# First feed-forward layer of a fused attention and mixing kernel: two blocks of hidden rows together, their 64-row products on two halves of the array

## The chip, the cores and the metric

The kernel runs on one core of one Trainium2 chip. The metric is the device time of one execution in microseconds. The time given for a kernel is the median of its runs. One execution was also recorded by the hardware profiler; the rows below are from it.

## What is computed

Three layers follow each other on `x` of shape (4, 4224, 192): a causal convolution with 7 taps for each head, a layer that mixes tokens with two 4224 x 4224 matrices, and a layer of rank-32 token mixing with a feed-forward network. The change touches the last one:

```python
def _moe2_ref(x, U, V, w_ch1, w_ch2):
    xt = x.transpose(0, 2, 1)
    h = xt @ U @ V
    u = x + h.transpose(0, 2, 1)
    ch = np.maximum(u @ w_ch1, 0.0) @ w_ch2
    return (u + ch).astype(np.float32)
```

`w_ch1` is 192 x 768, `w_ch2` 768 x 192. `d_model` is 192 = 128 + 64, so each contraction over it leaves 64 rows beside a full 128.

## The kernel before

The data lie transposed, features on the partitions and tokens along the free dimension. The four batches stand in two pairs (`p`). Of each pair the first batch's 128 rows are slot 0, the second's slot 2, and the two leftover 64 rows share slot 1, the first batch's in the upper half of the partitions (0 to 63), the second's in the lower half (64 to 127).

Every matrix product runs in fp32r, with each operand split into a high and a low part. A product is high by high, high by low and low by high, summed in PSUM. For the 64-row leftover, `parts_hi` and `parts_lo` build a slot (4 + b for batch b of the pair) that has the high part in one half and the low part in the other: high on top for b = 0, low on top for b = 1. The leftover weights stand in both halves, so one matmul over 128 rows gives (high + low) of the input by a weight.

Most of the span is the token mixing (`mix`, `group`, line 553). The feed-forward stage is the last sixth. `seq` lists its steps: 22 blocks `n` (11 chunks of 384 tokens by two pairs of batches), in each two batches `b`, in each six pieces `m` of 128 hidden rows, 264 steps in all. The order is written out by hand:

- `up(n, b, m)` makes one piece of the hidden layer: five matmuls of 384 columns into one PSUM bank of the pool `acc` (four banks, also used by `lift`): lines 818 and 819 the high weights by high and low input, 820 the low weights by high input, 821 the high leftover weights by slot 4 + b, 822 the low leftover weights by the same slot. ScalarE then takes the ReLU (824), VectorE the low part of it (825). `hid` has four buffers.
- `down`, two steps behind (`LAG`), multiplies the piece with the second layer: 840 and 841 into `ob`, 842 to 844 into `oa`.
- `lift` adds the rank-32 term to the input of the next block (one matmul, line 798, and an add on VectorE, line 800) at the steps in `LIFTS`: (0, 4), (0, 5) and (1, 0). `lift_split` splits that input: at b = 1, m = 1 `parts_hi` on ScalarE (603 to 605), at b = 1, m = 2 `parts_lo`, the large part on GpSimd (608), two small ones on VectorE (611, 614).
- `load_v` fetches and unpacks the next chunk of V. `finish` copies and adds the result (858, 859, 864, 870) and sends it out.
- `tail` holds what is left of the stage before and runs beside the first two steps: `m1[3]` transposes (665) and splits (669, 670), `m1[4]` multiplies with U (675), and `stack` prepares the rank-32 factor.

Of the kernel before, what the change touches and what calls it, by code (L numbers as in the profile page):

```python
# [10 lines left out]
F32 = mybir.dt.float32  # L11
F32R = mybir.dt.float32r
I32 = mybir.dt.int32
U16 = mybir.dt.uint16
AF = mybir.ActivationFunctionType
ALU = mybir.AluOpType
PSUM = bass.MemoryType.PSUM

P = 128
# [9 lines left out]
NM = DFF // P  # L29
BLOCKS = [1] * NS  # L30

COLS = 384
# [60 lines left out]
LIFTS = [(0, 4), (0, 5), (1, 0)]  # L93
# [20 lines left out]
def mix_kernel(ctx, tc, xT, wcv, wth, wtok, wch, uu, vv, w1, w2, outT):  # L114
    nc = tc.nc
    mm = nc.tensor.matmul

    def pool(name, bufs=1, side=None, space=None, stack=None):
        kw = dict(name=name, bufs=bufs, reuse_waits="tile")
        if side:  # L120
            kw["side"] = side
        if space is not None:
            kw["space"] = space
        return (stack or ctx).enter_context(tc.tile_pool(**kw))

    def f(ap):
        return ap.bitcast(F32)
# [47 lines left out]
    zp = pool("zp", bufs=4, side="right", stack=right)  # L175
    pp = pool("prep", side="right", stack=prep_st)
    ps_mm = pool("ps_mm", bufs=4, space=PSUM)
# [3 lines left out]
    y = [yt[:, :, o : o + w] for o, w in LATE]  # L181

    with tc.manual_schedule():
# [39 lines left out]
        n_chunks = len(pieces) // 2  # L223
# [20 lines left out]
        for h in range(2):  # L244
# [10 lines left out]
            out=wex, in0=wc_raw, in1=wmx.unsqueeze(2).to_broadcast([P, 2, TAPS]), op=ALU.subtract  # L255
# [10 lines left out]
            out=tap, in0=wex, in1=wsm.unsqueeze(2).to_broadcast([P, 2, TAPS]), op=ALU.mult  # L266
# [152 lines left out]
        def weight_part(t, g, q):  # L419

            if g < n_chunks:
                kb, n, _ = pieces[2 * g]
                if g >= n_chunks - len(LATE):

                    t = t[:, 8 : 8 + 4 * LSTEP]
                return t.rearrange("p (q k n) -> p q k n", q=2, k=2)[:, q, :kb, :n]

            return t[:, 2 * WSTEP * q + 16 : 2 * WSTEP * q + 16 + 2 * COLS]
# [172 lines left out]
        def parts_hi(q, src, p):  # L601

            nc.scalar.copy(q[0:64, 4, :], src[0:64, 3 * p + 1, :])
            nc.scalar.copy(q[64:128, 5, :], src[64:128, 3 * p + 1, :])
            nc.scalar.copy(q[:, 0:2, :], src[:, 3 * p : 3 * p + 3 : 2, :])  # L605
# [137 lines left out]
        m0, m1 = mixed[nmix - 2 :]  # L743
# [17 lines left out]
        c1 = (wh[n_chunks], wl[n_chunks])  # L761
# [6 lines left out]
        fo = pool("fin", stack=fin)  # L768
# [4 lines left out]
        def load_v(c, part):  # L773

            if c >= len(LATE):
                return
            if part == 0:
                vw = vraw[c] = vw_two[:, c % 2, :COLS, :]
                nc.sync.dma_start(out=vw, in_=v_columns(c))
            elif part == 1:  # L780
                unpack_parts(vraw[c])
            elif part == 2:
                unpack_join(vraw[c])
            else:
                v = late_fo["pool"].tile([P, COLS], F32R, name="vs", tag="vs", bufs=2)
                t = late_fo["pool"].tile([P, COLS], F32R, name="vt", tag="vt")
                split_v(c, words(vraw.pop(c), 1, F32), v, t)

        vraw = {}
        uq = {}  # L790

        def lift(n, j):

            if n >= nmix:
                return
            c, p = divmod(n, 2)
            h = ps_mm.tile([P, COLS], F32, name="acc", tag="acc")
            mm(h, pst[:, p, j * P : (j + 1) * P], vst[c], start=True, stop=True)
            d = y[c][:, 3 * p + j, :]
            nc.vector.tensor_tensor(out=d, in0=h, in1=d, op=ALU.add)  # L800

        def lift_split(n, part, eng=nc.gpsimd):
            if n >= nmix:
                return
            c, p = divmod(n, 2)
            if part == 0:
                uq[n] = zp.tile([P, 6, COLS], F32R, name="fq", tag="z")
                parts_hi(uq[n], y[c], p)
            else:
                parts_lo(uq[n], y[c], p, eng)  # L810

        hid = {}

        def up(n, b, m):
            q = uq[n]
            ps = ps_mm.tile([P, COLS], F32, name="acc", tag="acc")
            w = [weight_part(c1[part], n_chunks, h)[:, m * P : (m + 1) * P] for h in range(2) for part in range(2)]
            mm(ps, w[0], q[:, b, :], start=True, stop=False)  # L818
            mm(ps, w[0], q[:, 2 + b, :], start=False, stop=False)  # L819
            mm(ps, w[1], q[:, b, :], start=False, stop=False)  # L820
            mm(ps, w[2], q[:, 4 + b, :], start=False, stop=False)  # L821
            mm(ps, w[3], q[:, 4 + b, :], start=False, stop=True)  # L822
            h = hid[n, b, m] = fo.tile([P, 2, COLS], F32R, name="hid", tag="hid", bufs=4)
            nc.scalar.activation(h[:, 0, :], ps, AF.Relu)  # L824
            nc.vector.scalar_tensor_tensor(  # L825
                out=h[:, 1, :], in0=ps, scalar=0.0, in1=f(h[:, 0, :]), op0=ALU.max, op1=ALU.subtract
            )

        acc = {}

        def down(n, b, m):
            if m == 0:
                acc[n, b] = (
                    ps_p.tile([P, COLS], F32, name="oa", tag=f"acc{b}"),
                    ps_t.tile([P, COLS], F32, name="ob", tag="tr"),
                )
            oa, ob = acc[n, b]
            h = hid.pop((n, b, m))
            first, last = m == 0, m == NM - 1
            mm(ob, c2[:, m, 2, :], h[:, 0, :], start=first, stop=False)  # L840
            mm(ob, c2[:, m, 2, :], h[:, 1, :], start=False, stop=last)  # L841
            mm(oa, c2[:, m, 0, :], h[:, 0, :], start=first, stop=False)  # L842
            mm(oa, c2[:, m, 0, :], h[:, 1, :], start=False, stop=False)  # L843
            mm(oa, c2[:, m, 1, :], h[:, 0, :], start=False, stop=last)  # L844
# [4 lines left out]
        def finish(n, b, part):  # L849
            c, p = divmod(n, 2)  # L850
            if b == 0 and part == 0:
                outs[n] = late_fo["pool"].tile([P, 3, COLS], F32, name="ot", tag="ot", bufs=2)
            o = outs[n]
            oa, ob = acc[n, b]
            a, z = (0, 64) if b == 0 else (64, 0)
            dst = out3[:, 3 * p : 3 * p + 3, c * COLS : (c + 1) * COLS]
            if part == 0:
                nc.scalar.copy(o[a : a + 64, 1, :], ob[z : z + 64, :])
                nc.vector.tensor_tensor(
                    out=o[a : a + 64, 1, :], in0=ob[a : a + 64, :], in1=o[a : a + 64, 1, :], op=ALU.add  # L860
                )
            elif part == 1:
                if b == 1:
                    nc.vector.tensor_tensor(
                        out=o[:, 1, :], in0=o[:, 1, :], in1=y[c][:, 3 * p + 1, :], op=ALU.add
                    )
                    if n == nmix - 1:
                        nc.sync.dma_start(out=dst[:, 0:2], in_=o[:, 0:2, :])
            else:
                nc.vector.tensor_tensor(  # L870
                    out=o[:, 2 * b, :], in0=oa, in1=y[c][:, 3 * p + 2 * b, :], op=ALU.add
                )
                if b == 1:
                    first = 2 if n == nmix - 1 else 0
                    nc.sync.dma_start(out=dst[:, first:], in_=outs.pop(n)[:, first:, :])
# [9 lines left out]
        seq = [(n, b, m) for n in range(nmix) for b in range(2) for m in range(NM)]  # L885
        LAG = 2

        def post_done():
# [3 lines left out]
        tail = {  # L892
            0: [lambda: m1[4](0), lambda: m1[3](2)],
            1: [lambda: m1[4](1), lambda: m1[4](2), lambda: stack(1), post_done],
        }
        for i in range(len(seq) + LAG + 2):
            if i < len(seq):
                n, b, m = seq[i]
                up(n, b, m)
                for fn in tail.pop(i, ()):  # L900
                    fn()
                if n % 2 == 0 and b == 1 and m >= 3:
                    load_v(n // 2 + 1, m - 2)
                if n % 2 == 1 and b == 0 and m == 0:
                    load_v(n // 2 + 2, 0)
                if (b, m) in LIFTS:
                    lift(n + 1, LIFTS.index((b, m)))
                if b == 1 and m in (1, 2):
                    lift_split(n + 1, m - 1)
            if LAG <= i < len(seq) + LAG:  # L910
                down(*seq[i - LAG])
            for part in range(3):
                if 0 <= i - LAG - part < len(seq) and seq[i - LAG - part][2] == NM - 1:
                    finish(*seq[i - LAG - part][:2], part)
        fin.close()
        right.close()
        left.close()
# [62 lines left out]
```

## Time and profile before

| | |
|---|---|
| median of 3 runs | 3009.88 us (3009.52 to 3011.36) |
| profiled execution | 3011.35 us, its span 3009.6 us |
| mean granted TensorE clock | 0.995 |
| TensorE matmul, busy | 2960.8 us, 98% of the span |
| weight loads, busy | 2691.3 us, 89% |
| VectorE, busy | 2523.7 us, 84% |
| ScalarE, busy | 1570.8 us, 52% |
| GpSimd, busy | 275.3 us, 9% |
| feed-forward stage | about 2528 us to the end |

The profile is one execution of the program on the chip, times in microseconds from the start of the span. PE is TensorE's matmuls, PEld its weight loads, which overlap them, DVE is VectorE, ACT ScalarE, POOL GpSimd, SP SyncE. L822 is line 822 of the kernel. Matmuls are pipelined, and the ends of their records are modelled, so the distance of two starts says more than a record's length. Shares over the span average stages with different limits.

### The profile page before, as it was taken

Reading aid. Unit: us, or ns where it says so; the run is one execution under the profiler, and the core shown is the slowest. Engines: PE = TensorE matmul, PEld = TensorE weight load, DVE = VectorE, ACT = ScalarE, POOL = GpSimd, SP = SyncE. Lnnn points to the kernel's source line nnn. Section 1 sums busy time; section 2 is a strip of 40 time slices with the busy share of each in tenths; the row PEclk is TensorE's granted clock in tenths of the full one; section 3 lists DMA queues with packets and bytes.
Section 4 is the critical chain, followed back from the end, with each engine's and each line's share of the span. In section 5 each row is a group of like instructions: output and inputs, shape, how many; then the busy total and the mean of one; then the engine's idle time right before and its main releaser. Section 6 shows DMA issues by size and latency. Waiting matters only on the chain.

```text
span 3009.6 us, 38806 instructions
## 1 busy us (share of the span) xinstructions
PE 2960.8 (98%) x14884; PEld 2691.3 (89%) x14884; DVE 2523.7 (84%) x4147; ACT 1570.8 (52%) x2268; POOL 275.3 (9%) x245
## 2 busy tenths in 40 slices
PE   6999999999999999999999999999999998999999
PEld 5888888888888888888888888888889998999999
DVE  8799989898888888888989898889888997565655
ACT  7755555554555555454545454545455565444443
POOL 3210101000000000000001010000010000000000
PEclk9999999999999999999999999999999999999999
DMA  3433434343434343434343344333333221101110
GB/s 109 133 124 121 134 124 134 120 135 120 135 120 135 123 133 123 135 120 132 124 130 125 126 130 129 130 127 128 125 119 103 65 64 43 43 30 43 35 38 32
DMA packets 119002, 323.50 MB, mean 107 GB/s; under 512 B 6688, under 2 KB 40480, under 8 KB 118688
## 3 DMA queue, kind: packets, MB, share of 16 engines
q1 hardware_dynamic: 118816, 321.01, 33.1%
q8 instruction: 117, 1.92, 0.3%
q14 instruction: 69, 0.57, 0.1%
HBM read 308.01 MB, written 12.98 MB: 107 GB/s over the span
## 4 chain that ended last, share of the span: by engine, by line
PE 93%; DVE 4%; ACT 2%; issue 1%; DMA 0%; POOL 0%; DVEq 0%; POOLq 0%; ACTq 0%
PE acc L553 71%; PE ob L841 2%; PE ob L840 2%; PE oa L844 2%; PE oa L842 2%; PE acc L822 2%; PE acc L818 2%; PE acc L819 2%; PE acc L820 2%; PE oa L843 2%; PE acc L821 1%; DVE wraw L147 1%; PE pacc L675 1%; DVE wraw L150 1%; PE tr L665 1%; PE th L356 1%
## 5 line engine op out<-in xcount | busy, mean ns | idle before, releaser
L553 PE MATMUL acc<-whi,z 128*128 128x464 f32 (+2 forms) x7224 | 2131.4, 373 | 8.9 <-ACT yt L557 4.9
L553 PEld LDWEIGHTS acc<-whi,z 128*128 128x128 f32 x7224 | 1358.2, 188 | 174.8 <-ACT yt L557 7.6
L553 PE MATMUL acc<-wlo,z 128*128 128x464 f32 (+2 forms) x3612 | 1347.2, 373 | 3.0 <-POOL wlo L450 3.0
L553 PEld LDWEIGHTS acc<-wlo,z 128*128 128x128 f32 x3612 | 680.0, 188 | 89.8 <-POOL wlo L450 4.3
L559 DVE TENSOR_TENSOR yt<-acc,yt 128x464 f32<-128x464 f32 (+2 forms) x876 | 550.8, 634 | 221.9 <-PE acc L553 219.3
L447 ACT CAST whi<-wraw 128x928 fp32r<-128x928 f32 (+3 forms) x304 | 315.4, 1038 | 659.2 <-DVE wraw L150 658.9
L147 DVE TENSOR_SCALAR wraw<-wraw 128x928 uint16<-128x928 uint16 (+3 forms) x307 | 372.0, 1212 | 10.2 <-ACT wraw L143 6.1
L450 DVE TENSOR_TENSOR wlo<-wraw,whi 128x928 fp32r<-128x928 f32 (+2 forms) x290 | 371.8, 1282 | 1.0 <-ACT whi L447 1.0
L142 ACT ACTIVATE wraw<-wraw,consts 128x928 int32<-128x928 uint16 (+3 forms) x307 | 351.2, 1144 | 14.9 <-DMA wraw<-in_wtok 11.6
L150 DVE SCALAR_TENSOR_TENSOR wraw<-wraw 128x928 int32<-128x928 int32 (+3 forms) x307 | 344.9, 1123 | 10.6
L143 ACT ACTIVATE wraw<-wraw 128x928 f32<-128x928 f32 (+3 forms) x307 | 321.0, 1046 | 0.0
L316 DVE SCALAR_TENSOR_TENSOR xa<-xr,tap,xa 128x256 f32<-128x256 f32 (+1 forms) x768 | 301.6, 434 | 0.0
L403 POOL TENSOR_TENSOR z<-tz,z 128x384 fp32r<-128x384 f32 x120 | 123.9, 1032 | 1712.7 <-ACT z L400 1712.7
L825 DVE SCALAR_TENSOR_TENSOR hid<-acc,hid 128x384 fp32r<-128x384 f32 x264 | 146.8, 556 | 151.0 <-ACT hid L824 149.9
L824 ACT ACTIVATE hid<-acc 128x384 fp32r<-128x384 f32 x264 | 129.6, 491 | 255.0 <-PE acc L822 253.0
L400 ACT CAST z<-tz 128x384 fp32r<-128x384 f32 x130 | 66.7, 513 | 294.9 <-DVE tz L389 294.9
L818 PE MATMUL acc<-fq,whi 128*128 128x384 f32 x264 | 89.9, 341 | 5.5 <-ACT fq L605 5.5
L409 POOL TENSOR_TENSOR yt<-yt,xa 128x384 f32<-128x384 f32 x64 | 69.6, 1088 | 229.4 <-DVE xa L316 193.7
L844 PE MATMUL oa<-hid,cl 128*128 128x384 f32 x264 | 90.0, 341 | 0.0
L842 PE MATMUL oa<-hid,cl 128*128 128x384 f32 x264 | 89.8, 340 | 0.0
L840 PE MATMUL ob<-hid,cl 128*128 128x384 f32 x264 | 89.7, 340 | 0.0
L841 PE MATMUL ob<-hid,cl 128*128 128x384 f32 x264 | 89.7, 340 | 0.0
(216 smaller groups left out, 2792.0 us busy)
## 6 DMA issues: line engine op xcount, KB each, us to landing
wraw<-in_wtok SPq DMA_DIRECT2D x186, 928.0 KB, 4.7
wraw<-in_wtok SPq DMA_DIRECT2D x92, 960.0 KB, 4.9
wraw<-in_wtok SPq DMA_DIRECT2D x22, 768.0 KB, 4.3
xr<-in_xT SPq DMA_DIRECT2D x65, 201.0 KB, 2.6
outT<-ot SPq DMA_DIRECT2D x21, 576.0 KB, 2.9
vw<-in_vv SPq DMA_DIRECT2D x10, 384.0 KB, 3.9
wraw<-in_w SPq DMA_DIRECT2D x3, 768.0 KB, 4.3
ur<-in_uu SPq DMA_DIRECT2D x1, 1056.0 KB, 6.9
```

What stands on the lines that cost most here:

```text
L142: nc.scalar.activation(words(raw, 0), words(raw, 1, U16), AF.Identity, scale=2.0**-13, bias=consts[:, 3:4])
L143: nc.scalar.activation(words(raw, 1, F32), words(raw, 1, F32), AF.Copy, scale=2.0**-112)
L147: nc.vector.tensor_scalar(out=words(raw, 1, U16), in0=words(raw, 3, U16), scalar1=0x8000, scalar2=None, op0=ALU.bitwise_and)
L150: nc.vector.scalar_tensor_tensor(out=words(raw, 1), in0=words(raw, 1), scalar=3, in1=words(raw, 0), op0=ALU.logical_shift_left, op1=ALU.bi ...
L316: nc.vector.scalar_tensor_tensor(out=xa, in0=src, scalar=w, in1=xa, op0=ALU.mult, op1=ALU.add)
L447: nc.scalar.copy(hi, src)
L450: eng.tensor_tensor(out=weight_part(wl[g], g, q), in0=src, in1=f(hi), op=ALU.subtract)
L553: mm(ps, a, b[:, i + r, :], start=n == 0, stop=n == last)
L559: nc.vector.tensor_tensor(out=dst, in0=ps, in1=dst, op=ALU.add)
L818: mm(ps, w[0], q[:, b, :], start=True, stop=False)
L842: mm(oa, c2[:, m, 0, :], h[:, 0, :], start=first, stop=False)
L844: mm(oa, c2[:, m, 1, :], h[:, 0, :], start=False, stop=last)
```

## The change

`up` now takes two steps, m0 and m0 + 1. For each it runs the first four matmuls as before, into two banks. The fifth of each is now one over 64 rows: only the high part of the input by the low leftover weights, the first on the upper half of the array (rows 0 to 63), the second on the lower half (rows 64 to 127). Both read 384 columns and write all 128 partitions of their bank. Slot 4 + b has the high part in one half only, so the tile of a block gets a seventh slot with the high parts in the other halves, which two more ScalarE copies of 64 x 384 in `lift_split` fill. ReLU and low part of both pieces come after all ten matmuls. The loop goes in steps of two: `up` for a pair, then what stood beside the first and the second (`beside`), then `down` and `finish` for the two steps of the pair before. The low by low product of the leftover rows, which before came along in L822, is no longer computed.

```diff
--- before.py
+++ after.py
@@ -804,27 +804,35 @@
                 return
             c, p = divmod(n, 2)
             if part == 0:
-                uq[n] = zp.tile([P, 6, COLS], F32R, name="fq", tag="z")
-                parts_hi(uq[n], y[c], p)
+                q = uq[n] = zp.tile([P, 7, COLS], F32R, name="fq", tag="z")
+                parts_hi(q, y[c], p)
+                nc.scalar.copy(q[64:128, 6, :], y[c][0:64, 3 * p + 1, :])
+                nc.scalar.copy(q[0:64, 6, :], y[c][64:128, 3 * p + 1, :])
             else:
                 parts_lo(uq[n], y[c], p, eng)
 
         hid = {}
 
-        def up(n, b, m):
+        def up(n, b, m0):
             q = uq[n]
-            ps = ps_mm.tile([P, COLS], F32, name="acc", tag="acc")
-            w = [weight_part(c1[part], n_chunks, h)[:, m * P : (m + 1) * P] for h in range(2) for part in range(2)]
-            mm(ps, w[0], q[:, b, :], start=True, stop=False)
-            mm(ps, w[0], q[:, 2 + b, :], start=False, stop=False)
-            mm(ps, w[1], q[:, b, :], start=False, stop=False)
-            mm(ps, w[2], q[:, 4 + b, :], start=False, stop=False)
-            mm(ps, w[3], q[:, 4 + b, :], start=False, stop=True)
-            h = hid[n, b, m] = fo.tile([P, 2, COLS], F32R, name="hid", tag="hid", bufs=4)
-            nc.scalar.activation(h[:, 0, :], ps, AF.Relu)
-            nc.vector.scalar_tensor_tensor(
-                out=h[:, 1, :], in0=ps, scalar=0.0, in1=f(h[:, 0, :]), op0=ALU.max, op1=ALU.subtract
-            )
+            sums = []
+            for m in (m0, m0 + 1):
+                ps = ps_mm.tile([P, COLS], F32, name="acc", tag="acc")
+                w = [weight_part(c1[part], n_chunks, h)[:, m * P : (m + 1) * P] for h in range(2) for part in range(2)]
+                mm(ps, w[0], q[:, b, :], start=True, stop=False)
+                mm(ps, w[0], q[:, 2 + b, :], start=False, stop=False)
+                mm(ps, w[1], q[:, b, :], start=False, stop=False)
+                mm(ps, w[2], q[:, 4 + b, :], start=False, stop=False)
+                sums.append((ps, w[3]))
+            for t, (ps, w) in enumerate(sums):
+                r = slice(64 * t, 64 * t + 64)
+                mm(ps, w[r], q[r, 4 + b if t == b else 6, :], start=False, stop=True)
+            for t, (ps, _) in enumerate(sums):
+                h = hid[n, b, m0 + t] = fo.tile([P, 2, COLS], F32R, name="hid", tag="hid", bufs=4)
+                nc.scalar.activation(h[:, 0, :], ps, AF.Relu)
+                nc.vector.scalar_tensor_tensor(
+                    out=h[:, 1, :], in0=ps, scalar=0.0, in1=f(h[:, 0, :]), op0=ALU.max, op1=ALU.subtract
+                )
 
         acc = {}
 
@@ -893,25 +901,30 @@
             0: [lambda: m1[4](0), lambda: m1[3](2)],
             1: [lambda: m1[4](1), lambda: m1[4](2), lambda: stack(1), post_done],
         }
-        for i in range(len(seq) + LAG + 2):
-            if i < len(seq):
-                n, b, m = seq[i]
-                up(n, b, m)
-                for fn in tail.pop(i, ()):
-                    fn()
-                if n % 2 == 0 and b == 1 and m >= 3:
-                    load_v(n // 2 + 1, m - 2)
-                if n % 2 == 1 and b == 0 and m == 0:
-                    load_v(n // 2 + 2, 0)
-                if (b, m) in LIFTS:
-                    lift(n + 1, LIFTS.index((b, m)))
-                if b == 1 and m in (1, 2):
-                    lift_split(n + 1, m - 1)
-            if LAG <= i < len(seq) + LAG:
-                down(*seq[i - LAG])
-            for part in range(3):
-                if 0 <= i - LAG - part < len(seq) and seq[i - LAG - part][2] == NM - 1:
-                    finish(*seq[i - LAG - part][:2], part)
+        def beside(i):
+            n, b, m = seq[i]
+            for fn in tail.pop(i, ()):
+                fn()
+            if n % 2 == 0 and b == 1 and m >= 3:
+                load_v(n // 2 + 1, m - 2)
+            if n % 2 == 1 and b == 0 and m == 0:
+                load_v(n // 2 + 2, 0)
+            if (b, m) in LIFTS:
+                lift(n + 1, LIFTS.index((b, m)))
+            if b == 1 and m in (1, 2):
+                lift_split(n + 1, m - 1)
+
+        for i0 in range(0, len(seq) + LAG + 2, 2):
+            if i0 < len(seq):
+                up(*seq[i0])
+                for i in (i0, i0 + 1):
+                    beside(i)
+            for i in (i0, i0 + 1):
+                if LAG <= i < len(seq) + LAG:
+                    down(*seq[i - LAG])
+                for part in range(3):
+                    if 0 <= i - LAG - part < len(seq) and seq[i - LAG - part][2] == NM - 1:
+                        finish(*seq[i - LAG - part][:2], part)
         fin.close()
         right.close()
         left.close()
```

## Rows read from the trace of the kernel before

**Rows 1.** The page: busy us (share of the span) and instructions of an engine.
```profile
PE 2960.8 (98%) x14884; PEld 2691.3 (89%) x14884; DVE 2523.7 (84%) x4147; ACT 1570.8 (52%) x2268; POOL 275.3 (9%) x245
```

**Rows 2.** Three stretches of the feed-forward stage: length, busy times (instructions), granted clock, DMA.
```profile
2600.00:2700.00 100.00, 100.00 (x575) 100.00 (x574) 58.19 (x109) 44.58 (x88) 9.26 (x5) 1.00 0.11 38
2700.00:2800.00 100.00, 100.00 (x574) 100.00 (x573) 58.20 (x110) 43.10 (x85) 7.42 (x4) 1.00 0.12 42
2800.00:2900.00 100.00, 100.00 (x575) 100.00 (x574) 59.22 (x111) 47.36 (x93) 9.27 (x5) 1.00 0.09 33
```

**Rows 3.** Who waited for whom, 2600 to 2900 us: us in total, times, longest.
```profile
POOL fq L608 <- ACT fq L605: 274.8, 14, 19.8
ACT hid L824 <- PE acc L822: 159.4, 140, 1.4
DVE hid L825 <- ACT hid L824: 92.8, 112, 1.2
```

**Rows 4.** Instructions in order of time, one step: start us, length us, engine, line.
```profile
2780.12 0.33 PE L821 MATMUL acc<-fq,whi 128*128 128x384 f32 x1
2780.29 0.34 PE L822 MATMUL acc<-fq,wlo 128*128 128x384 f32 x1
2780.29 0.19 PEld L840 LDWEIGHTS ob<-hid,cl 128*128 128x128 f32 x1
2780.46 0.34 PE L840 MATMUL ob<-hid,cl 128*128 128x384 f32 x1
...
2780.66 0.49 ACT L824 ACTIVATE hid<-acc 128x384 fp32r<-128x384 f32 x1 [1.42 <-PE acc L822]
```

**Rows 5.** Weight loads of two lines: ns min/median/max, first and last start us.
```profile
L822 PEld LDWEIGHTS acc<-fq,wlo x264: 187/188/330, 2530.0 to 3001.4; 128*128 128x128 f32 x132
...
L675 PEld LDWEIGHTS pacc<-u2s,cz x132: 133/137/223, 2299.4 to 2533.8; 128*64 128x64 f32 x132
```

**Rows 6.** In order of time: L675 (64 columns) between transposes; x3 merges three.
```profile
2303.67 0.49 PE L665 MATMUL tr<-ident,yt 128*128 128x128 f32 x3
2303.91 0.59 PE L675 MATMUL pacc<-u2s,cz 128*64 128x384 f32 x2
2304.34 0.49 PE L665 MATMUL tr<-ident,yt 128*128 128x128 f32 x3
2304.58 0.42 PE L553 MATMUL acc<-whi,z 128*128 128x384 f32 x1
2304.84 0.34 PE L553 MATMUL acc<-wlo,z 128*128 128x384 f32 x1
...
2303.67 0.25 PEld L665 LDWEIGHTS tr<-ident,yt 128*128 128x128 f32 x2
...
2304.16 0.34 PE L675 MATMUL pacc<-u2s,cz 128*64 128x384 f32 x1
```

**Rows 7.** The group of all L675: count, busy us, mean ns, idle before.
```profile
L675 PE MATMUL pacc<-u2s,cz 128*64 128x384 f32 x132 | 38.6, 370 | 3.1 <-DVE u2s L670 2.8 <-ACT u2s L669 0.3
```

**Rows 8.** What writes the split input fq: ns min/median/max, first and last start us.
```profile
L603 ACT CAST fq<-yt x22: 499/506/515, 2526.3 to 2974.4; 64x384 fp32r<-64x384 f32 x22
L604 ACT CAST fq<-yt x22: 507/511/511, 2526.8 to 2974.9; 64x384 fp32r<-64x384 f32 x22
L605 ACT CAST fq<-yt x22: 832/837/837, 2527.3 to 2975.4; 128x768 fp32r<-128x768 f32 x22
...
L608 POOL TENSOR_TENSOR fq<-yt,fq x21: 1836/1854/1857, 2546.7 to 2976.4; 128x768 fp32r<-128x768 f32 x21
```

**Rows 9.** Groups, 2600 to 2900 us: count, busy us, mean ns, idle before.
```profile
L825 DVE SCALAR_TENSOR_TENSOR hid<-acc,hid 128x384 fp32r<-128x384 f32 x168 | 93.5, 556 | 93.5 <-ACT hid L824 92.8
L824 ACT ACTIVATE hid<-acc 128x384 fp32r<-128x384 f32 x168 | 82.5, 491 | 160.8 <-PE acc L822 159.4
...
L800 DVE TENSOR_TENSOR yt<-acc,yt 128x384 f32<-128x384 f32 x42 | 23.0, 547 | 0.0
...
L858 ACT COPY ot<-ob 64x384 f32<-64x384 f32 x28 | 13.3, 474 | 0.7
```

**Rows 10.** In order of time, the start of the feed-forward stage, TensorE.
```profile
2528.21 0.69 PE L818 MATMUL acc<-fq,whi 128*128 128x384 f32 x1 [5.51 <-ACT fq L605]
...
2531.34 0.84 PE L665 MATMUL tr<-ident,yt 128*128 128x128 f32 x3
...
2533.42 0.85 PE L675 MATMUL pacc<-u2s,cz 128*64 128x384 f32 x4
```

## What the change is predicted to do, before it was run

> **What bounds the kernel now.** I read the share of each engine first, then stretches of the stage that the diff touches, then who waited for whom there, then single instructions. TensorE is busy for 98% of the span [rows 1], but that number alone says little, so the stage decides. The feed-forward stage runs from about 2528 us to the end. Three stretches of 100 us from its middle show TensorE with no gap, at a granted clock of 1.00 (2.4 GHz), VectorE at 58 to 59% and ScalarE at 43 to 47% [rows 2]. In the list of waits of the same 300 us TensorE doesn't appear as a waiter; ScalarE waits for its products, and GpSimd for ScalarE [rows 3]. So in this stage time is the number of matmul slots times the length of a slot. The rows with 575, 574 and 575 matmuls in 100 us each give 0.174 us a slot, and two neighbours start 2780.29 and 2780.46 [rows 2, 4]. A weight load starts together with the matmul before it (the load of L840 at 2780.29, with the matmul of L822) and is hidden in it [rows 4].
>
> **The part that is to gain.** A step (one of 12 pieces of 128 hidden rows for a pair of batches) is five slots in up and five in down. The fifth in up (L822) multiplies the low part of the leftover 64 weight rows with high and low parts of the input, though only the high part matters. The change makes it a product of 64 rows, and runs those of two neighbouring steps in the two halves of the array. There are 264 steps, so 132 pairs, and for each pair two slots of 0.174 us become one shared stretch. Were the two products exactly side by side, 132 x 0.174 = 22.9 us would go.
>
> The trace of before has no matmul on 64 rows, so what the shared stretch costs has to be bounded. Three things can spoil it: the second weight load, a changeover between the full and the halved array, and that the halves don't overlap at all.
>
> *The second load.* Loads of 128 columns last 188 ns and of 64 columns 137 ns [rows 5]; the difference, 51 ns for 64 columns, makes 102 ns for 128, the rest being a fixed delay. The three short transposes say the same from another side: their loads and matmuls follow each other every 0.11 us, although 128 columns at 2.4 GHz stream in 0.053 us [rows 6]. So a load holds its path for 0.102 us, and a matmul can follow its load by 0.11 us. Take T as the start of the last full product of the pair. If both loads go one after the other from T, the upper half's matmul starts at T+0.174 (when the full one is through), the lower half's at T+0.102+0.110 = T+0.212. It streams until T+0.386, and the load for L840, which needs both halves, starts at T+0.212 and is ready at T+0.322, in time. L840 starts at T+0.386 where it starts at T+0.522 today: 0.136 us saved a pair, 18.0 us in all. If the second load must wait until the first half's matmul has begun, as every load of before waits for the matmul ahead of it [rows 4], the lower half starts at T+0.174+0.110 = T+0.284 and L840 at T+0.458: 0.064 us saved, 8.4 us. I take the first: the load of the lower half touches no weights that the upper half's matmul needs, whereas in before every load writes where the next but one would.
>
> *The changeover.* The nearest rows are the products of L675, which fill only 64 columns and stand between transposes of the full array [rows 6]. From the third transpose (about 2303.89, as the rows put the three 0.11 apart) to the second L675 at 2304.16 is 0.27 us, and 0.11 + 0.174 = 0.28 is what two slots need without any changeover; from there to the next transpose is 0.18, an ordinary slot; and back at L553 the two starts 2304.84 minus about 2304.56 are 0.28 again. Over all 132 of them the records are 370 ns long against 340 ordinarily, 4 us in total, with 3.1 us of idle time [rows 7]. So changing the number of columns costs about nothing here. It is a change of columns and not of rows, so it isn't proof, and the other end of the bound is an empty array: a matmul record is 0.34 us from start to written result [rows 4], so a changeover that waits for the last result costs 0.34 - 0.174 = 0.166 us, twice a pair. I take zero, by L675, and keep the other end as a rival.
>
> Here two rules of the Trainium skill stand against each other. TensorEngine Tiling (Array Packing), section Tiling Modes, states that changing the tiling mode, as against only the tile, drains TensorE; by that rule the changeover would be paid twice a pair, and L675 shows nothing of the kind, though no run here has yet changed the number of rows. TensorE: Matmul & The Clock Gate, Part 3, has small tiles start about 4 ns apart; by that figure the estimate would be 132 x (0.174 - 0.004) = 22.4 us.
>
> **What it adds beside TensorE.** Two copies of 64x384 on ScalarE for each of 22 blocks, at 0.51 us as L603 and L604 [rows 8], 22.4 us in all, in an engine that is over half idle in this stage [rows 2]. I cost them at nothing, and follow them where the queue is fullest: the pair b=1, m=0 and 1. Count from its first matmul. Eight full slots end at 1.39, the ReLU starts 0.37 after its product's start (2780.29 to 2780.66 [rows 4]), so two ReLUs of 0.49 end at about 2.75; VectorE's two subtractions of 0.56 end at 3.4 and the add of the third lift at 3.95 [rows 9]. L605 waits for that add, since lift and copies now stand in one iteration, so ScalarE does L603 and L604 until 3.8, L605 (0.84) until 4.8, the new copies until 5.8 and L858 (0.47) until 6.3 [rows 8, 9]. The next pair's first ReLU was ready at 5.3: it is 1.0 late, and its hidden tile is complete at about 7.4. TensorE wants that tile after one more pair, at about 8.6. GpSimd's L608 (1.85) [rows 8] starts at 4.8 and ends at 6.7, and the next block's first product comes at about 10. So 1.2 us are left. Were that cover gone, up to 22 x 1.0 = 22 us would show.
>
> Taking two pieces together also makes PSUM tighter. Each iteration takes two of the four acc banks, and three lifts in six iterations take one each. The tightest spot is the pair after the first two lifts, which takes the banks of the pair before: their last reader ends at 3.4, TensorE comes back at 1.6 + 2 x 0.174 + 10 x 0.174 = 3.7. 0.3 us are left, and each 0.1 us missing would cost 2.2 us over 22 blocks. SyncE's transfers (load_v and the output) and GpSimd's queue keep their order; they move by one step at most, and none is waited for here [rows 3].
>
> At the start of the stage there is a small loss. Today five matmuls stand between the transposes of L665 and the four L675 that need their result (2531.34 and 2533.42 [rows 10]). With ten products ahead of both, only two L675 (0.35 to 0.65 us) stand between, while ReLU 0.49, ReLU 0.49, copy 0.48 and a subtraction of 0.56 come before the result is there. TensorE waits about 1 us once (0 to 2 us). The first L818 still waits only for L605, since the new copies stand behind it [rows 8, 10]. At the end nothing changes: the last pair's second hidden tile is ready about 2.0 us after its product begins and used after 2.8.
>
> **The sum.** -18.0 + 1.0 = -17.0 us. The profiled execution took 3011.35 us, 3009.6 of it span, which is 1.5 us over the median of three; so 2994.4 us against it, and 2993 us against the median of 3009.88.
>
> **Rivals.** All from the median. (a) The loads overlap entirely, or a little better than I have it: -22.9 + 1.0, 2988; I count it into the forecast, whose own range is 2986 to 2998. (b) The second load waits for the first half's matmul: -8.4 + 1.0, 3002.5. For it speaks that no load of before runs two ahead [rows 4]. (c) The halves don't overlap and the 64 rows cost a whole slot each: 3011, so the change wouldn't do what it says. Nothing in the trace speaks against it, as before has no such pair. (d) The slower side: each changeover waits until the array is empty. The halves then start at T+0.340 and L840 at T+0.680, 0.158 us later than today; 132 x 0.158 + 1.0 = 21.9 us, 3032. It decides from 0.087 us a changeover, at which the gain of 0.174 is eaten up. Against it speaks L675, for it that a whole product's result leaves the array 0.34 us after its start while the halves would already be taking over [rows 4, 6]. This is what the page on tiling named above would lead to. (e) The loads wait for the empty array too: T+0.340, both loads until T+0.55, empty again at T+0.89, a load, T+1.00: 0.48 us a pair, 3074.
>
> **How the numbers follow.** Chances: forecast with (a) 0.38, (b) 0.17, (c) 0.17, (d) 0.20, (e) 0.08. The slower cases hold 0.28, more than 2 in 10, so the range reaches to (d) and leaves out (e) alone: 2986 to 3034. It covers the unknown price of a changeover between zero and an emptied array. About 0.2%, 6 us, is what a measurement here can tell from no change. Faster takes the forecast and most of (b): 0.53. The same takes (c) and the rest of (b): 0.19. Slower is (d) and (e): 0.28.
>
> **What would show it.** In a profile after, the last product of a pair's first half and of the second should start about 0.04 us apart, and L840 0.17 after the second; 0.11 apart means (b), 0.17 apart (c). A gap of more than 0.2 us ahead of the first or behind the second means (d), and loads that begin only behind that gap (e). In the middle of the stage 300 us hold 168 steps today [rows 9], 3.571 us a pair; they should hold 175, 3.435 us a pair. Waits of TensorE for ScalarE or VectorE once a block would show that the copies or the banks were mis-costed, and a wait of about 1 us near 2533 us the loss at the start. The prediction fails first with the changeover, which no row of before can price.

## The result, and the profile after

The changed kernel takes 3037.93 us (median of 4, 3036.38 to 3039.07), the kernel before 3009.78 us: a ratio of 1.0091, with a 95% interval of 1.0078 to 1.0104. It is 28.2 us slower. The forecast was 2993 us, and the time lies above the range, between the rivals (d), 3032, and (e), 3074. The profiled execution took 3036.38 us, 3034.6 of it span.

The stretches of the feed-forward stage, with the columns of [rows 2], show fewer matmuls in the same time, at the same clock of 1.00, and weight loads busy for 88% where they were busy throughout:

```profile
2600.00:2700.00 100.00, 100.00 (x545) 88.77 (x544) 53.49 (x105) 43.05 (x90) 7.32 (x4) 1.00 0.11 38
2700.00:2800.00 100.00, 100.00 (x544) 88.33 (x543) 52.74 (x103) 46.05 (x95) 9.18 (x5) 1.00 0.09 32
2800.00:2900.00 100.00, 100.00 (x545) 88.77 (x544) 52.41 (x103) 43.37 (x91) 7.32 (x4) 1.00 0.09 32
```

TensorE's busy share is still 100%, so it hides the loss. The records of matmuls reach over it. The loss is in the share of the loads, and in the list of waits of 2600 to 2900 us (us in total, times, longest), where the weight loads now wait, for nothing that the profile names:

```profile
ACT hid L832 <- PE acc L829: 145.4, 60, 3.2
...
PEld acc L829 <- issue: 19.4, 79, 0.2
...
PEld ob L848 <- issue: 9.9, 53, 0.2
...
PEld acc L798 <- issue: 4.8, 26, 0.2
```

79 pairs lie in these 300 us. 79 times the loads of the 64-row products (L829) wait 0.25 us, and 79 times (53 + 26) the load behind them does, 0.19 us. TensorE itself waits for ScalarE or VectorE nowhere. One pair in order of time, matmuls first, then loads (start us, length us):

```profile
2783.41 0.33 PE L824 MATMUL acc<-fq,wlo 128*128 128x384 f32 x1
2783.58 0.34 PE L825 MATMUL acc<-fq,whi 128*128 128x384 f32 x1
2783.85 0.44 PE L829 MATMUL acc<-fq,wlo 64*128 64x384 f32 x2
2784.22 0.44 PE L848 MATMUL ob<-hid,cl 128*128 128x384 f32 x1
2784.50 0.34 PE L849 MATMUL ob<-hid,cl 128*128 128x384 f32 x1
...
2783.41 0.19 PEld L825 LDWEIGHTS acc<-fq,whi 128*128 128x128 f32 x1
2783.85 0.19 PEld L829 LDWEIGHTS acc<-fq,wlo 64*128 64x128 f32 x2 [0.25 <-issue]
2784.22 0.19 PEld L848 LDWEIGHTS ob<-hid,cl 128*128 128x128 f32 x1 [0.18 <-issue]
2784.33 0.19 PEld L849 LDWEIGHTS ob<-hid,cl 128*128 128x128 f32 x1
```

Ordinarily a load starts with the matmul before it, as the load of L825 does at 2783.41 with L824, and as in [rows 4]. The loads of L829 start 0.27 us after the last full product (2783.58 to 2783.85). Their matmuls have records of 0.44 us where 0.33 is ordinary: I read this as 0.11 us in which they stand ready and wait for the weights, so that they really start at 2783.96. From there it is 0.26 us to the load of L848 (2784.22), and L848 too is 0.11 us too long. So the way in costs 0.27 + 0.11 = 0.38 us and the way out 0.26 + 0.11 = 0.37, each where a slot is 0.174. From L825 to L849 it is 0.92 us where four slots took 4 x 0.174 = 0.696: 0.224 us more, times 132 pairs 29.6 us.

That the two halves overlap is seen in the groups of the same 300 us (count, busy us, mean ns, idle before), first of the matmuls, then of the loads:

```profile
L829 PE MATMUL acc<-fq,wlo 64*128 64x384 f32 x158 | 35.0, 440 | 0.0
```

```profile
L829 PEld LDWEIGHTS acc<-fq,wlo 64*128 64x128 f32 x158 | 14.7, 183 | 19.4 <-issue 19.4
```

158 records of 440 ns would fill 69.5 us one after another, and cover 35.0, which is 79 x 0.443: the two of a pair coincide. The loads do the same: 158 x 0.183 = 28.9 us, covering 14.7.

The stage now begins so:

```profile
2525.79 0.69 PE L822 MATMUL acc<-fq,whi 128*128 128x384 f32 x1 [4.56 <-ACT fq L605]
```

From the first product of the stage to the end it is 3034.6 - 2525.8 = 508.8 us, before 3009.6 - 2528.2 = 481.4 [rows 10]: 27.4 us more, so the whole loss is in this stage. (The spans of the two profiled executions differ by 25.0 us, since the stage began 2.4 us earlier; in the kernels of this document it begins anywhere from 2525.3 to 2528.3.) It is a little under 29.6 since ordinary slots became shorter by about 1.3 ns: from L849 at 2780.81 to the second L825 at 2783.58 it is 2.77 us for 16 slots, before, from L842 at 2780.82 to L821 at 2783.61, 2.79. Times 132 that is about 2.6 us; the start of the stage, below, takes about 1 us of it back.

### The profile page after: what moved, and what is told of

It is laid out like the page before. It is cut to its first block, busy times and chain, and to the rows that moved or that the text cites. A ratio compares the mean times of both kernels' runs of the same rounds, so it can differ in the third digit from the quotient of the medians.

```text
span 3034.6 us, 38891 instructions
## 1 busy us (share of the span) xinstructions
PE 2987.2 (98%) x14884; PEld 2660.3 (88%) x14884; DVE 2511.7 (83%) x4147; ACT 1581.9 (52%) x2312; POOL 274.3 (9%) x245
## 4 chain that ended last, share of the span: by engine, by line
PE 93%; DVE 4%; ACT 2%; issue 0%; POOL 0%; DMA 0%; SPq 0%; DVEq 0%; ACTq 0%; POOLq 0%
PE acc L553 71%; PE ob L848 2%; PE acc L829 2%; PE acc L825 2%; PE acc L823 2%; PE acc L824 2%; PE ob L849 2%; PE acc L822 2%; PE oa L851 2%; PE oa L852 2%; PE oa L850 2%; DVE wraw L147 1%; DVE wraw L150 1%; PE pacc L675 1%; PE tr L665 1%; PE acc L798 1%
## 5 line engine op out<-in xcount | busy, mean ns | idle before, releaser
L833 DVE SCALAR_TENSOR_TENSOR hid<-acc,hid 128x384 fp32r<-128x384 f32 x264 | 135.0, 553 | 164.9 <-ACT hid L832 164.4
L832 ACT ACTIVATE hid<-acc 128x384 fp32r<-128x384 f32 x264 | 115.3, 489 | 244.0 <-PE acc L829 243.1
L848 PE MATMUL ob<-hid,cl 128*128 128x384 f32 x264 | 98.1, 372 | 0.0
L822 PE MATMUL acc<-fq,whi 128*128 128x384 f32 x264 | 89.2, 338 | 4.6 <-ACT fq L605 4.6
L825 PE MATMUL acc<-fq,whi 128*128 128x384 f32 x264 | 89.5, 339 | 0.0
L823 PE MATMUL acc<-fq,whi 128*128 128x384 f32 x264 | 88.8, 337 | 0.3 <-DVE fq L608 0.3
L824 PE MATMUL acc<-fq,wlo 128*128 128x384 f32 x264 | 89.1, 337 | 0.0
```

## The experiments

The theory was now: each change between full array and halved array (a changeover) costs 0.20 us beyond a slot, two make a visit of 0.40, and what is inside a visit runs as hoped. The first rival: it is the order by pairs. The second: it is the 64-row products themselves, two at once, with a second bank and a seventh slot, and not the changeovers.

**Pairs with full products.** The changed kernel with the fifth product over 128 rows again:

```diff
-                mm(ps, w[r], q[r, 4 + b if t == b else 6, :], start=False, stop=True)
+                mm(ps, w, q[:, 4 + b, :], start=False, stop=True)
```

> The order by pairs and the two extra copies stay, but the fifth product of each step runs over all 128 rows again. Theory (changeover: each change between the full and the halved array costs about 0.20 us, whatever else was changed): no changeover is left, so 3010 to 3012 us, at most the 1 to 2 us of the start. Rival (order: pairing the steps, later ReLUs or the tighter banks make the loss): 3030 us or more, with TensorE waiting for ScalarE or VectorE once a block.

Measured: 3008.95 us against 3010.55 before, ratio 0.9995 (0.9986 to 1.0005). The order, the two copies and the tighter banks cost nothing that can be measured. (The kernel before was run beside each group of experiments; its medians lie between 3009.78 and 3011.05 us, so a difference between kernels of two groups is sure to about 1.3 us.) Its stretches hold 577 matmuls each against 575, so the slightly shorter slots come with the order by pairs, for a reason that no run shows:

```profile
2600.00:2700.00 100.00, 100.00 (x577) 100.00 (x576) 56.41 (x112) 47.48 (x98) 9.28 (x5) 1.00 0.11 38
```

**One 64-row product at a time.** The kernel before with one edit, no pairs, no second bank:

```diff
-            mm(ps, w[3], q[:, 4 + b, :], start=False, stop=True)
+            r = slice(64 * b, 64 * b + 64)
+            mm(ps, w[3][r], q[r, 4 + b, :], start=False, stop=True)
```

> The kernel before with one edit: the fifth product runs on the 64 rows that hold the high part, alone, step by step, nothing beside it; the low by low product of the leftover rows is left out. Theory: 264 visits to the halved array, two changeovers each, 264 x 0.40 = 106 us, so about 3115 us. Rival (the loss comes from running two halves at once, two banks or the seventh slot): 3010 us. Rival (order): 3010 us.

Measured: 3115.79 us, ratio 1.0352 (1.0335 to 1.0369). 105.2 us over 264 visits is 0.399 us a visit. The same waits stand around a lone product, matmuls first, then loads:

```profile
2780.20 0.34 PE L821 MATMUL acc<-fq,whi 128*128 128x384 f32 x1
2780.47 0.44 PE L823 MATMUL acc<-fq,wlo 64*128 64x384 f32 x1
2780.84 0.44 PE L841 MATMUL ob<-hid,cl 128*128 128x384 f32 x1
2781.13 0.34 PE L842 MATMUL ob<-hid,cl 128*128 128x384 f32 x1
...
2780.47 0.18 PEld L823 LDWEIGHTS acc<-fq,wlo 64*128 64x128 f32 x1 [0.25 <-issue]
2780.84 0.19 PEld L841 LDWEIGHTS ob<-hid,cl 128*128 128x128 f32 x1 [0.19 <-issue]
```

From L821 to L842 it is 0.93 us, where three slots are 0.52: 0.41 us. Both rivals fall.

**Both products in the same half.**

```diff
-                r = slice(64 * t, 64 * t + 64)
-                mm(ps, w[r], q[r, 4 + b if t == b else 6, :], start=False, stop=True)
+                r = slice(64 * b, 64 * b + 64)
+                mm(ps, w[r], q[r, 4 + b, :], start=False, stop=True)
```

> The changed kernel with both 64-row products of a pair on the same half of the array, so that they can't overlap. Theory: still one visit a pair, but two slots in it in place of one shared one: 132 x 0.174 = 23 us over the changed kernel, about 3061 us. Rival (the halves never overlapped in the changed kernel): the same 3038 us.

Measured: 3059.57 us, ratio 1.0164 (1.0148 to 1.0179), 21.6 us over the changed kernel, 0.164 us a pair. This is what overlap in the changed kernel was worth, and nearly the 0.174 of a slot. The records of the two matmuls together now cover 0.62 us where they covered 0.44.

**The halves twice.** The pair of 64-row products runs twice in one visit:

```diff
-            for t, (ps, w) in enumerate(sums):
-                r = slice(64 * t, 64 * t + 64)
-                mm(ps, w[r], q[r, 4 + b if t == b else 6, :], start=False, stop=True)
+            for last in (False, True):
+                for t, (ps, w) in enumerate(sums):
+                    r = slice(64 * t, 64 * t + 64)
+                    mm(ps, w[r], q[r, 4 + b if t == b else 6, :], start=False, stop=last)
```

> The changed kernel with the two 64-row products of a pair run twice in a row, in the same visit (the leftover high by low product is added twice). Theory: the visit's fixed price stays, and one more shared stretch costs a slot, 132 x 0.174 = 23 us over the changed kernel, about 3061 us. Rival (each stretch of 64-row products pays again what the first one pays over the slots): 132 x (0.17 + 0.40) = 75 us over it, 3113 us.

Measured: 3061.34 us, ratio 1.0167 (1.0152 to 1.0183), 23.4 us over the changed kernel, 0.177 us for one more shared stretch. Within a visit a stretch costs a slot and nothing else; the price hangs on the visit.

**Groups of four.** `up` takes the steps as four and two, then two and four, and makes the 64-row products of a group in one visit (two shared stretches in a group of four). `down` runs a group behind, with five hidden buffers in place of four; of the edit, the lines that make the groups:

```diff
-            for m in (m0, m0 + 1):
+            for m in ms:
...
-                r = slice(64 * t, 64 * t + 64)
-                mm(ps, w[r], q[r, 4 + b if t == b else 6, :], start=False, stop=True)
+                r = slice(64 * (t % 2), 64 * (t % 2) + 64)
+                mm(ps, w[r], q[r, 4 + b if t % 2 == b else 6, :], start=False, stop=True)
...
+            for ms in (((0, 1, 2, 3), (4, 5)) if b == 0 else ((0, 1), (2, 3, 4, 5)))
...
```

> The same 64-row products in the same two halves, but taken in groups of four and two steps in place of two, two and two (five hidden buffers in place of four): 88 visits to the halved array in place of 132. Theory: 44 visits fewer, 44 x 0.40 = 18 us under the changed kernel, about 3020 us. Rival (the cost goes with the number of 64-row products and not of visits): 3038 us. If the four banks become too tight, TensorE waits for ScalarE or VectorE, and the time lies above 3020 us.

Measured: 3040.22 us, ratio 1.0100 (1.0085 to 1.0115): no gain, though a third of the visits is gone. Its waits from 2600 to 2900 us show why, 13 blocks with a wait that no kernel had before:

```profile
PEld acc L829 <- issue: 13.1, 53, 0.2
PEld acc L825 <- DVE fq L611: 11.6, 13, 0.9
...
PE acc L825 <- DVE fq L611: 7.5, 13, 0.6
```

and in order of time, at the start of a block, the third and fourth product of the first step, then what VectorE did ahead of them:

```profile
2780.00 0.34 PE L824 MATMUL acc<-fq,wlo 128*128 128x384 f32 x1
2780.92 0.44 PE L825 MATMUL acc<-fq,whi 128*128 128x384 f32 x1 [0.58 <-DVE fq L611]
...
2778.33 1.95 DVE L833 SCALAR_TENSOR_TENSOR hid<-acc,hid 128x384 fp32r<-128x384 f32 x4 [0.80 <-ACT hid L832]
2780.31 0.55 DVE L611 TENSOR_TENSOR fq<-yt,fq 64x384 fp32r<-64x384 f32 x1
```

53 visits have their 0.25 us in 300 us, but once a block TensorE waits for the leftover's low part: 0.92 us where a slot is 0.174. Those small subtractions (L611, L614) stand on VectorE behind the four subtractions of a whole group (L833). The wait comes 21 times in the run, at every block but the first, and 21 x 0.75 = 15.7 us ate most of what 44 visits fewer gave back.

**Groups of four, the split earlier.** The one edit against it puts both parts of the split ahead of the group of four:

```diff
-            if b == 1 and m in (1, 2):
-                lift_split(n + 1, m - 1)
+            if b == 1 and m == 1:
+                lift_split(n + 1, 0)
+                lift_split(n + 1, 1)
```

> The groups of four and two again, with one edit: both parts of the next block's split are issued before the group of four, so that the two small subtractions (L611, L614) no longer stand behind its four ReLU subtractions on VectorE. In the kernel before this edit TensorE waits for L611 in each block, 0.75 us between L824 and L825 over a slot, and starts the stage with about 2.5 us of waits. Theory: the waits in the blocks go, 22 x 0.75 = 16.5 us, and what stays is the changed kernel less 44 visits of 0.40 us and plus the start, 3020 to 3024 us. Rival (the cost goes with the number of 64-row products): the wait goes and another takes its place, or the time stays over 3035 us.

Measured: 3022.36 us against 3011.05 before (median of seven runs), ratio 1.0040 (1.0025 to 1.0055), inside the expected 3020 to 3024. TensorE waits for nothing in 300 us, and the visits stand as counted:

```profile
PEld acc L829 <- issue: 13.4, 54, 0.2
```

Its three stretches hold 563, 565 and 563 matmuls against 545, 544 and 545; with 123 in a block (120 of the steps, three lifts) a block takes 21.8 us against 22.6, 0.76 less where two visits fewer should give 0.80. In all it is 15.6 us under the changed kernel, 0.35 us for each of the 44 visits, where 0.40 makes 17.6. The start of the stage takes a part back. TensorE waits there for the split behind the transposes (L675) and for the lift's rank-32 factor (L798), some 2.5 us where the changed kernel has 0.2:

```profile
2535.05 0.39 PE L675 MATMUL pacc<-u2s,cz 128*64 128x384 f32 x1 [0.80 <-ACT u2s L669]
2535.98 0.39 PE L675 MATMUL pacc<-u2s,cz 128*64 128x384 f32 x1 [0.55 <-DVE u2s L670]
...
2539.30 0.59 PE L798 MATMUL acc<-vz,cl 128*128 128x384 f32 x2 [1.16 <-DVE cl L696]
```

17.6 - 2.3 = 15.3 us were due, and 15.6 were measured. With the visit's price it adds up from the other side too: a visit of one shared stretch loses 0.40 - 0.174 = 0.226, one of two 0.40 - 0.348 = 0.052; 44 of each make 12.2 us over before, and 11 to 13 were measured (against the kernel before of this group or of the first).

**Fewer columns, and 96 rows.** Two edits of the kernel before ask which change of shape makes a changeover:

```diff
-            mm(ps, w[1], q[:, b, :], start=False, stop=False)
+            mm(ps[0:64, :], w[1][:, 0:64], q[:, b, :], start=False, stop=False, skip_group_check=True)
```

> The kernel before with one edit: the third product of each step (low weights by high input) uses 64 of its 128 weight columns, over all 128 rows; half of that product is left out. Were every change of the array's shape a changeover of 0.20 us, 264 x 0.40 = 106 us would come on top, 3115 us. If it is only the rows, 3010 us, as L675 showed.

```diff
-            mm(ps, w[3], q[:, 4 + b, :], start=False, stop=True)
+            mm(ps, w[3][0:96], q[0:96, 4 + b, :], start=False, stop=True)
```

> The kernel before with one edit: the fifth product runs over rows 0 to 95 in place of 0 to 127; part of the leftover product is left out. If any product with fewer rows makes a changeover: 3115 us. If only one that fits half of the array does: 3010 us.

Measured: 3011.37 us with 64 columns, ratio 1.0003 (0.9993 to 1.0013), and 3009.46 with 96 rows, 0.9999 (0.9990 to 1.0008). Neither makes one. In order of time, the kernel with 64 columns:

```profile
2781.39 0.33 PE L819 MATMUL acc<-fq,whi 128*128 128x384 f32 x1
2781.56 0.34 PE L820 MATMUL acc<-fq,wlo 128*64 128x384 f32 x1
2781.74 0.34 PE L821 MATMUL acc<-fq,whi 128*128 128x384 f32 x1
```

and the one with 96 rows:

```profile
2781.48 0.33 PE L821 MATMUL acc<-fq,whi 128*128 128x384 f32 x1
2781.65 0.34 PE L822 MATMUL acc<-fq,wlo 96*128 96x384 f32 x1
2781.83 0.34 PE L840 MATMUL ob<-hid,cl 128*128 128x384 f32 x1
```

All of these are ordinary slots of 0.17 to 0.18 us. So what makes a changeover is neither fewer columns nor fewer rows as such; of what was run, only products on 64 rows, in one half of the array, make one. Products on 32 rows were not run.

## Why the prediction was wrong

**The changeover is the step that failed.** "I take zero, by L675". L675 was read rightly: 264 products of 64 columns a run cost nothing either. But it changes columns, and the price goes with the half of the rows. I had written that it isn't proof, and still gave it the forecast. The visit costs 0.40 us: by the lone products, 105.2 us for 264 visits, 132 cost 52.6 us, against 22.9 us that the shared slots save. That is 29.7 us, and 28.2 were measured. The rule of the Trainium skill, TensorEngine Tiling (Array Packing), Tiling Modes, that changing the mode drains TensorE, was the better guide: the trace agrees for products on 64 rows, at 0.20 us a change. For products on 64 columns or on 96 rows no run shows such a cost.

**The bound from the other end had the right kind and wrong parts.** For (d) I let each changeover wait for a whole record, 0.34 us from start to start, with loads hidden: 0.166 us beyond a slot. In the trace the loads start 0.26 to 0.27 us after the product, 0.09 us after its slot's end, and not 0.166. But then a load lies open before each first matmul, 0.11 us. Together 0.20. The size of that load, 0.11 us, was in my working, from the transposes [rows 6]; (d) left it out. (e) had it in, but with the long wait and with two loads one after the other, and came to 0.48 us a pair where 0.224 was measured. By the signs that I had set, loads that begin only behind the gap mean (e), and here they begin only behind a wait: the kind is that of (e), the rival with the smallest chance, at about half its loss. The range ended at (d), 4 us short. That the time lies near (d) is chance: a shorter wait and an open load, each wrong in (d), nearly make up for each other.

**The second load was wrong too, without harm.** I had loads of the two halves one after the other, the lower half 0.04 us behind the upper. They run at the same time, and so do the matmuls. Only with both products in one half does the second load come about 0.1 us later (two loads together 0.29 us against 0.19). The figure that Part 3 of TensorE: Matmul & The Clock Gate, in the Trainium skill, gives for starts of small tiles, about 4 ns apart, fits: both records of a pair start in the same hundredth of a microsecond. Had the changeover been free, (a) with 22.9 us would have been the closer sum; the runs with one half (0.164 us) and with one more stretch (0.177 us) price the slot at 0.17 as used.

**What held.** The stage is bound by slots, and loss and gain are counted in them. The copies, the late ReLUs and the banks are covered: TensorE has no wait in the middle of the stage, and pairs with full products take the time of before. The start loses about as much as was said, but only in part as was said: from the first product of the stage to that of the third step it is 7.1 us where it was 5.9. The list of waits has 0.2 us for L675 there and not 1. In the same stretch lies one visit at a granted clock of 0.50 (1.2 GHz), and that clock lasts until 6.3 us after the first product, where before it lasted 5.0 us; so the size that came out is partly luck. The spare time on VectorE was no safe ground for larger groups: one wait of 0.75 us a block ate about 16 us when four ReLU subtractions came in a row.

## What to carry to other kernels

Going from products on the whole array to products on 64 rows and back costs 0.40 us at the granted clock of 1.00, in fp32r with 128 weight columns and 384 moved columns, in every form that was run: one product, two at once, two in one half, two stretches. Count visits before counting saved slots. With slots of 0.174 us a visit would pay from three shared stretches, six 64-row products, on; this is an estimate from 0.174 and 0.40, and no run had three. Here six steps in one visit would win 3 x 0.174 - 0.40 = 0.12 us, 5 us in all by estimate from these runs, but would need six accumulator banks beside those of the second layer, where this kernel has four; that wasn't tried. A neighbour in the trace that looks like the new operation settles nothing if it differs in the very thing that is new, here columns against rows.

## What the hardware showed that was not expected

Where a full product is followed by a 64-row one, the next weight load starts only 0.27 us after the product's start, and about the same on the way back (0.26 us); ordinarily the load starts with that product. 64 columns out of 128, and 96 rows out of 128, cost nothing of the kind (ratios 1.0003 and 0.9999). Weights for both halves load at the same time, two in 0.19 us, and two for the same half in 0.29. And the busy share of the matmuls shows none of it: it stood at 100% in all kernels but the groups of four with their wait, while weight loads fell from 100% to 88%, and to 80% with 264 visits. A lower share of the loads alone proves no loss, though: with 64 columns it fell to 98% too, because each of those loads lasts 134 ns in place of 188, and the time stayed the same.

```profile
2600.00:2700.00 100.00, 100.00 (x574) 97.85 (x573) 58.71 (x110) 44.63 (x88) 9.25 (x5) 1.00 0.11 38
```
